# Preparation of weights and of v, held in its queue behind the step of g that precedes it in the source

## The chip, the core and the metric

The kernel runs on one core of a Trainium2 chip. The metric is the device time of one execution in microseconds (us), here the median of the runs shown. A core has TensorE (matrix products), VectorE, ScalarE and GpSimd (work on tiles), SyncE (starts most transfers) and DMA engines that carry them. Each engine works through its own queue of instructions in order; an instruction that has to wait holds up all that stand behind it in that queue.

## The reference

An attention over pooled keys and values feeds a gated layer, and that a second layer (4608 tokens of 512):

```python
k_p = k.reshape(B, H, Sp, pool, D).mean(axis=3)          # pool = 8: 576 keys become 72
v_p = v.reshape(B, H, Sp, pool, D).mean(axis=3)
scores = scale * np.matmul(q, k_p.transpose(0, 1, 3, 2))
scores = scores - np.max(scores, axis=-1, keepdims=True)
attn = np.exp(scores)
attn = attn / (np.sum(attn, axis=-1, keepdims=True) + 1e-09)
x = np.matmul(attn, v_p)              # then laid out as [B * S, H * D] = [4608, 512]
a = x @ w1; b = x @ w2                # 512 -> 1024
x = ((a * b) @ w3) @ w_out            # 1024 -> 1024 -> 512
h = x @ w_in                          # 512 -> 2048
r = np.maximum(h, 0.0); g = r * r
out = g @ w_out2                      # 2048 -> 512
```

## The kernel before, in words

Every product of 32-bit numbers is made of three matmuls on rounded halves: an operand is written as hi (rounded) plus lo (the rounded rest), and hi x hi, hi x lo and lo x hi are summed. Rounding thus costs one copy on ScalarE (hi) and one difference on VectorE (lo), here `split` (lines 119 and 120 in the profile) or lines of its own.

In the first 105 us `fold` multiplies w3 by the first w_out into one matrix W, Wt in the profile. Then, up to 828 us, nine blocks of 512 tokens run through the first layer. Each has eight steps: `stage_ab` makes the sums with w1 and w2 (ps_w) and from them the step of g: `asb`, ScalarE's copy of the sum with w1; `gf`, VectorE's product with the other sum; `gt`, the rounding of gf. `stage_w`, two steps later, multiplies gt by W into the sums acc. The attention of the eight batches is spread between these matmuls: scores ps_s, exp (att, line 482), the rest rem of a group, transposes ps_t that are rounded to aT and aR, and the products ps_av with the rounded pooled v (vl, and vr for what does not fill 128 rows), from which x is rounded (lines 543 and 546).

The second layer follows from 818 us. Its products are made in Strassen's manner, with seven products of quarters in place of eight, for four pairs of blocks and a plain ninth block: `h_step` multiplies x2o by units of weights, un, that are fetched from memory into a ring of eight. Its quarters of weights, their sums and differences are prepared beforehand and stored. One set of this preparation (`make_quarters`) loads two tiles (raw or rq), turns each with two scalings on ScalarE (`words`, lines 150 and 151) and three operations on VectorE (`join`, lines 159 to 162) into wq, makes the sums sq (lines 896 to 900), rounds all into oq (lines 910 and 914) and stores them. `second_half` does the like for the second halves of w1 and w2 (w32, wt2, lines 1289 and 1293) and `parted` rounds v (lines 359 and 360). The operands of the first pair, x2o, are rounded from x2r, which is loaded (line 1059) from the outputs x2d of the first layer; `cut` makes some differences of x2r first (line 1071).

raw, rq, x2r and the tiles of k and v share a pool of three buffers. wq, sq and oq share one of four. A load waits until the last reader of the buffer's old content is done, and it waits in SyncE's queue, in front of all that stand behind it.

The source issues all of this in one interleaved order (`tick` lets a pump issue a next piece of attention or of preparation after every six matmuls), but it does not fix the queues: a scheduler orders each engine's queue by the dependencies and its own model of when things get ready. An edge without a semaphore can be added between two instructions of one engine, as `issue_after` does: the first then has to stand ahead of the other. Before, `behind` uses this alone for the sums that pool k and v (lines 322 and 326), which stand behind `front["dve"]`, the last gf or Wt of the source.

## Time and profile before

| | us |
|---|---|
| median of 3 runs | 1529.75 (1527.83 to 1531.23) |
| the profiled execution | 1530.1, of which the trace spans 1528.3 |
| TensorE busy | 1488.6 (97%) |
| VectorE busy | 1001.5 (66%) |
| ScalarE busy | 798.3 (52%) |
| GpSimd busy | 83.6 (5%) |

A busy TensorE is one with a matmul in flight; weights are loaded beside that. The profile gives for each engine the idle time ahead of an instruction and what ended it. `issue` there means that the profile shows nothing that it waited for. The granted clock is 1.00 where TensorE ran at 2.4 GHz and 0.50 where it ran at 1.2 GHz.

### The profile page before, as it was taken

How to read it: one execution, taken by the hardware profiler on the slowest of the kernel's cores; microseconds unless marked ns; L12 is line 12 of the kernel's file. 1: busy time of each engine (PE TensorE's matmuls, PEld its weight loads, DVE VectorE, ACT ScalarE, POOL GpSimd, SP SyncE). 2: the span in 40 equal slices, each digit the busy share in tenths (PEclk: the TensorE clock that was granted, in tenths of full speed). 3: DMA queues.
4: the chain of work that ended last, by engine and by line, in shares of the span. 5: the costliest groups of instructions: out<-in, count | busy, mean ns of one | idle time of the engine just before them, and what ended most of it. 6: DMA issues, size and time to landing. Idle time of an engine off the chain costs nothing.

```text
span 1528.3 us, 21310 instructions
## 1 busy us (share of the span) xinstructions
PE 1488.6 (97%) x6752; PEld 1197.6 (78%) x6752; DVE 1001.5 (66%) x1798; ACT 798.3 (52%) x1953; POOL 83.6 (5%) x144
## 2 busy tenths in 40 slices
PE   5899999999999999999999999999999999999998
PEld 3457778787888887878888878888888888888887
DVE  7988686667757467657255476759675967576542
ACT  6866464454635345546244574457445744464441
POOL 1011111111110011100000000000000000000000
PEclk9999999999999999999999999999999999999999
DMA  9544666667676557648439777778777777798752
GB/s 295 190 139 138 165 201 164 188 158 203 169 198 177 172 130 211 205 140 263 136 126 306 217 203 231 207 209 231 235 207 206 234 206 207 207 268 283 209 162 90
DMA packets 292783, 301.34 MB, mean 197 GB/s; under 512 B 119360, under 2 KB 184896, under 8 KB 292672
## 3 DMA queue, kind: packets, MB, share of 16 engines
q1 hardware_dynamic: 287488, 290.54, 65.9%
q10 hardware_dynamic: 5184, 9.44, 1.7%
q8 instruction: 55, 0.90, 0.3%
q14 instruction: 56, 0.46, 0.1%
HBM read 243.27 MB, written 56.62 MB: 196 GB/s over the span
## 4 chain that ended last, share of the span: by engine, by line
PE 78%; DVE 10%; DMA 4%; ACT 4%; issue 2%; SPq 1%; ACTq 0%; DVEq 0%
PE ps_w L192 21%; PE o L1202 18%; PE acc L192 10%; PE ps_a L1100 5%; PE ps_c L1100 5%; PE ps_d L1100 5%; PE ps_h L192 3%; PE o L192 3%; PE ps_b L1100 3%; PE ps_s L465 2%; PE ps_av L192 1%; ACT att L482 1%; DVE gt L120 1%; DVE vp L326 1%; DVE raw L160 1%
## 5 line engine op out<-in xcount | busy, mean ns | idle before, releaser
L1202 PE MATMUL o<-gt,un 128*128 128x512 f32 x1344 | 330.1, 390 | 1.4 <-DVE gt L120 1.0
L1202 PEld LDWEIGHTS o<-gt,un 128*128 128x128 f32 x1344 | 251.8, 188 | 56.0 <-DVE gt L120 3.5
L120 DVE TENSOR_TENSOR gt<-gs,gt 128x512 fp32r<-128x512 f32 x240 | 164.7, 689 | 183.1 <-ACT gt L119 181.6
L192 PE MATMUL ps_w<-x,wt 128*128 128x512 f32 x960 | 243.5, 399 | 1.7 <-DVE x L546 0.9
L119 ACT CAST gt<-gs 128x512 fp32r<-128x512 f32 x240 | 148.6, 620 | 154.5 <-PE o L1202 89.3
L192 PE MATMUL acc<-gt,Wt 128*128 128x512 f32 x864 | 216.3, 394 | 0.0
L192 PEld LDWEIGHTS ps_w<-x,wt 128*128 128x128 f32 x960 | 175.7, 189 | 40.8 <-DVE x L546 2.6
L192 PEld LDWEIGHTS acc<-gt,Wt 128*128 128x128 f32 x864 | 159.9, 188 | 31.9
L192 PE MATMUL ps_w<-x,un 128*128 128x512 f32 x768 | 184.3, 393 | 0.0
L192 PEld LDWEIGHTS ps_w<-x,un 128*128 128x128 f32 x768 | 142.7, 188 | 29.6 <-issue 0.4
L482 ACT ACTIVATE att<-ps_s,mx 128x72 f32<-128x72 f32 (+1 forms) x320 | 97.9, 323 | 50.4 <-DVE mx L480 50.0
L1107 ACT ACTIVATE r<-r 128x512 f32<-128x512 f32 x96 | 60.7, 632 | 118.4 <-DVE r L1137 117.9
L827 DVE TENSOR_TENSOR gf<-asb,ps_w 128x512 f32<-128x512 f32 x72 | 49.3, 684 | 83.7 <-PE ps_w L192 75.2
L1100 PE MATMUL ps_a<-x2o,un 128*128 128x512 f32 x384 | 98.0, 390 | 0.1
L1100 PE MATMUL ps_c<-x2o,un 128*128 128x512 f32 x384 | 97.6, 390 | 0.0
L1100 PE MATMUL ps_d<-x2o,un 128*128 128x512 f32 x384 | 97.5, 389 | 0.0
L1108 ACT ACTIVATE gs<-r 128x512 f32<-128x512 f32 x144 | 90.0, 629 | 4.3 <-DMA x2r<-x2d 2.6
L1176 DVE TENSOR_TENSOR gs<-gs 128x512 f32<-128x512 f32 x128 | 86.6, 684 | 0.0
L119 ACT CAST gt<-gf 128x512 fp32r<-128x512 f32 x72 | 44.9, 623 | 75.4 <-DVE gf L827 75.3
L1100 PEld LDWEIGHTS ps_a<-x2o,un 128*128 128x128 f32 x384 | 72.0, 188 | 15.5 <-ACT p L1125 0.6
L1100 PEld LDWEIGHTS ps_c<-x2o,un 128*128 128x128 f32 x384 | 72.0, 188 | 15.2 <-DVE u L1131 0.3
L1100 PEld LDWEIGHTS ps_d<-x2o,un 128*128 128x128 f32 x384 | 72.1, 188 | 15.0
(113 smaller groups left out, 1969.5 us busy)
## 6 DMA issues: line engine op xcount, KB each, us to landing
un<-u_w SPq DMA_DIRECT2D x128, 256.0 KB, 3.2
un<-u_A SPq DMA_DIRECT2D x128, 256.0 KB, 3.0
un<-u_S SPq DMA_DIRECT2D x128, 256.0 KB, 3.0
un<-u_oS SPq DMA_DIRECT2D x128, 256.0 KB, 3.0
un<-u_oA SPq DMA_DIRECT2D x96, 256.0 KB, 3.0
raw<-in_moe_w_dram SPq DMA_DIRECT2D x32, 512.0 KB, 5.2
raw<-in_moe_w_out_dram SPq DMA_DIRECT2D x24, 512.0 KB, 4.5
kv<-in_k_dram SPq DMA_DIRECT2D x32, 256.0 KB, 3.4
```

The lines of the kernel that those rows point to most:

```text
L119: nc.scalar.copy(hi, src)
L120: return (eng or nc.vector).tensor_sub(lo, src, f32(hi))
L160: nc.vector.scalar_tensor_tensor(u, hi, 0x80000000, lo, op0=ALU.bitwise_and, op1=ALU.bitwise_or)
L192: (lambda a=a, b=b, i=i: nc.tensor.matmul(ps, a, b, start=first and i == 0, stop=last and i == n - 1))
L465: nc.tensor.matmul(ps[:n, x * 2 * SP:(x + 1) * 2 * SP], t[:, hp, c0:c0 + n], kbd[:, hp].rearrange("p a s -> p (a s)"), start=True, stop=True)
L482: nc.scalar.activation(av[:, h0 + h], sv[:, h], ACTF.Exp, bias=mx[:n, h:h + 1], scale=scale, accum_out=sm[:n, h0 + h:h0 + h + 1])
L827: front["dve"] = nc.vector.tensor_mul(gf, asb, pss[1])
L1100: nc.tensor.matmul(ps, l, r, start=first and j == 0, stop=j == len(todo) - 1, skip_group_check=True)
L1107: nc.scalar.activation(t, src, ACTF.Relu)
L1108: nc.scalar.activation(take(name), t, ACTF.Square)
L1176: d = nc.vector.tensor_sub(src, a, src)
L1202: nc.tensor.matmul(ob[x][o], l, r, start=u == 0 and m != 5 and j == 0, stop=u == NU - 1 and j == 2, skip_group_check=True)
```

## The change

`front` gets a second entry, for ScalarE, and `behind` is called with the engine. `front["act"]` is the last asb copy, and after it the hi copy of gt; `front["dve"]` is the last gf (or Wt), and after it the lo difference of gt. The scalings, the first instruction of each join, the roundings of v but for line 372, the sums of a set (the first of each half) and the roundings of wt2 and oq get an edge behind the entry that stands there when the source issues them. The rounding of gt is written out, without `split`, so that its two instructions can be entered. In the profile after, lines from 150 on stand one to three further down.

```diff
-    def behind(ins):
-
-        if "dve" in front:
-            issue_after(ins, front["dve"])
+    def behind(ins, eng="dve"):
+
+        if eng in front:
+            issue_after(ins, front[eng])
+        return ins
...
-        nc.scalar.activation(hf, hf, ACTF.Copy, scale=2.0 ** -112)
-        nc.scalar.activation(w.bitcast(U32), r[:, :, 0], ACTF.Copy, scale=2.0 ** -29)
+        behind(nc.scalar.activation(hf, hf, ACTF.Copy, scale=2.0 ** -112), "act")
+        behind(
+            nc.scalar.activation(w.bitcast(U32), r[:, :, 0], ACTF.Copy, scale=2.0 ** -29), "act")
...
-        nc.vector.tensor_scalar(lo, hi, 3, None, op0=ALU.logical_shift_left)
+        behind(nc.vector.tensor_scalar(lo, hi, 3, None, op0=ALU.logical_shift_left))
...
-            nc.scalar.activation(hi, src, ACTF.Copy, scale=row)
-            nc.vector.scalar_tensor_tensor(
-                lo, src, row, f32(hi), op0=ALU.mult, op1=ALU.subtract)
+            behind(nc.scalar.activation(hi, src, ACTF.Copy, scale=row), "act")
+            behind(nc.vector.scalar_tensor_tensor(
+                lo, src, row, f32(hi), op0=ALU.mult, op1=ALU.subtract))
...
-                nc.scalar.copy(asb, ps)
+                front["act"] = nc.scalar.copy(asb, ps)
...
         front["dve"] = nc.vector.tensor_mul(gf, asb, pss[1])
-        split(gt[:, 0, :], gt[:, 1, :], gf)
+        front["act"] = nc.scalar.copy(gt[:, 0, :], gf)
+        front["dve"] = nc.vector.tensor_sub(gt[:, 1, :], gf, f32(gt[:, 0, :]))
...
-                nc.vector.tensor_add(s1, a21, quarter(w, 1, 1))
+                behind(nc.vector.tensor_add(s1, a21, quarter(w, 1, 1)))
...
-                nc.vector.tensor_sub(s3, a11, a21)
+                behind(nc.vector.tensor_sub(s3, a11, a21))
...
-            nc.scalar.copy(order(t[:, 0, :]), natural(part(n)))
+            behind(nc.scalar.copy(order(t[:, 0, :]), natural(part(n))), "act")
...
-            nc.vector.tensor_sub(
-                order(t[:, 1, :]), natural(part(n)), order(f32(t[:, 0, :])))
+            behind(nc.vector.tensor_sub(
+                order(t[:, 1, :]), natural(part(n)), order(f32(t[:, 0, :]))))
...
-            nc.scalar.copy(t[:, 0, :], st_["w"])
+            behind(nc.scalar.copy(t[:, 0, :], st_["w"]), "act")
...
-            nc.vector.tensor_sub(t[:, 1, :], st_["w"], f32(t[:, 0, :]))
+            behind(nc.vector.tensor_sub(t[:, 1, :], st_["w"], f32(t[:, 0, :])))
```

What this does to the queues is seen at three places. Numbers behind a name tell one buffer's use from another.

First place, ScalarE's queue near 300 us of the trace, before: two scalings of a weight's second tile, rq_2922, stand ahead of the attention's rounding aT0_2892 and its exps (att).

```order
L150 ACTIVATE rq_2919<-rq_2919 128x512
L151 ACTIVATE wq_3014<-rq_2919 128x512
L482 ACTIVATE att1_105,sm_2947<-ps_s_2943,mx_2946 128x72 x4
L910 CAST oq_3108<-wq_3014 128x512
L823 COPY asb_2972<-ps_w1_2954 128x512
L150 ACTIVATE rq_2922<-rq_2922 128x512
L151 ACTIVATE wq_3014<-rq_2922 128x512
L119 CAST aT0_2892<-ps_t_3003 128x4x128
L482 ACTIVATE att1_105,sm_2947<-ps_s_2987,mx_2990 128x72 x4
L119 CAST gt_3018<-gf_3017 128x512
```

The same stretch of ScalarE's queue in the changed kernel.

```order
L484 ACTIVATE att1_105,sm_2947<-ps_s_2943,mx_2946 128x72 x4
L825 COPY asb_2972<-ps_w1_2954 128x512
L151 ACTIVATE rq_2919<-rq_2919 128x512
L153 ACTIVATE wq_3014<-rq_2919 128x512
L830 CAST gt_3018<-gf_3017 128x512
L119 CAST aT0_2892<-ps_t_3003 128x4x128
L484 ACTIVATE att1_105,sm_2947<-ps_s_2987,mx_2990 128x72 x4
L859 COPY st_3025<-acc0_2240 128x512
L859 COPY st_3031<-acc1_2241 128x512
L860 DMA x2d1_107<-st_3025 128x512
```

The scalings of rq_2922 have left the stretch (they stand twelve rows further down, behind another group of exps); those of rq_2919 and gt_3018 stand ahead of aT0_2892 now, and the rounding oq_3108 has gone down as well.

Second place, VectorE before: the joins of set 5's tiles raw_7798 and raw_7800 into wq_8015, during the attention of the last batch, some 100 us before the first layer ends.

```order
L914 TENSOR_TENSOR oq_7774<-sq_7711,oq_7774 128x4x4x32
L914 TENSOR_TENSOR oq_7796<-sq_7711,oq_7796 128x4x4x32
L159 TENSOR_SCALAR raw_7798<-raw_7798 128x512
L160 SCALAR_TENSOR_TENSOR raw_7798<-raw_7798 128x2x256
L159 TENSOR_SCALAR raw_7800<-raw_7800 128x512
L162 ISA wq_8015<-raw_7798,wq_8015 128x1024
L160 SCALAR_TENSOR_TENSOR raw_7800<-raw_7800 128x2x256
L162 ISA wq_8015<-raw_7800,wq_8015 128x1024
L914 TENSOR_TENSOR oq_8079<-wq_8015,oq_8079 128x4x4x32
```

VectorE in the changed kernel, around the same joins.

```order
L831 TENSOR_TENSOR gt_8042<-gf_8041,gt_8042 128x512
L161 TENSOR_SCALAR raw_7798<-raw_7798 128x512
L162 SCALAR_TENSOR_TENSOR raw_7798<-raw_7798 128x2x256
L161 TENSOR_SCALAR raw_7800<-raw_7800 128x512
L164 ISA wq_8015<-raw_7798,wq_8015 128x1024
L162 SCALAR_TENSOR_TENSOR raw_7800<-raw_7800 128x2x256
L164 ISA wq_8015<-raw_7800,wq_8015 128x1024
L120 TENSOR_TENSOR x2o_7831<-x2r_7853,x2o_7831 128x512
L1074 TENSOR_TENSOR x2r_7850<-x2r_7853,x2r_7850 128x512
L120 TENSOR_TENSOR x2o_7832<-x2r_7830,x2o_7832 128x512
L829 TENSOR_TENSOR gf_8104<-asb_8085,ps_w2_8087 128x512
L120 TENSOR_TENSOR x2o_7823<-x2r_7856,x2o_7823 128x512
```

They now stand behind the last step of g but one (gt_8042), and the roundings of the second layer's operands (x2o) and the differences of x2r stand behind them. Before, all x2o of this list stood at least 20 rows ahead of gt_8042.

SyncE before: the loads of x2r_7853 and x2r_7856 into the buffers that these joins read, with the stores of set 4 (u_oS) ahead of them.

```order
L961 DMA u_oS3_4_8011<-oq_7796 256x1x256
L961 DMA u_oS4_4_8013<-oq_7796 256x1x256
L1059 DMA x2r_7853<-x2d0_106 128x512
L1059 DMA x2r_7853<-x2d1_107 128x512
L1059 DMA x2r_7856<-x2d0_106 128x512
L1059 DMA x2r_7856<-x2d1_107 128x512
L961 DMA u_oA11_5_8154<-oq_8079 256x1x256
```

SyncE in the changed kernel, with those loads and the fetches (un) of the second layer's units around them.

```order
L964 DMA u_oS3_4_8011<-oq_7796 256x1x256
L964 DMA u_oS4_4_8013<-oq_7796 256x1x256
L234 DMA un_8018<-u_A11_0_2201 128x512
L234 DMA un_8020<-u_S2_0_2494 128x512
L234 DMA un_8037<-u_S1_0_2490 128x512
L234 DMA un_8039<-u_S3_0_2532 128x512
L1062 DMA x2r_7853<-x2d0_106 128x512
L1062 DMA x2r_7853<-x2d1_107 128x512
L1062 DMA x2r_7856<-x2d0_106 128x512
L1062 DMA x2r_7856<-x2d1_107 128x512
L234 DMA un_8081<-u_A12_0_2286 128x512
L234 DMA un_8083<-u_S4_0_2536 128x512
```

Six fetches stand between the stores and the loads now that came after the loads before, and further fetches stand behind them.

Third place, TensorE near 680 us before: the attention's products ps_av_6942 between matmuls of W on gt_6822.

```order
L192 MATMUL acc0_6441<-gt_6822,Wt_994 128x512 x2
L192 MATMUL ps_av_6942<-aT0_6692,vl_101 128x256
L192 MATMUL ps_av_6942<-aT1_6693,vl_101 128x256
L465 MATMUL ps_s_6952<-kbd_103,qT_6320 128x144 x2
L192 MATMUL acc0_6441<-gt_6822,Wt_994 128x512
L192 MATMUL acc1_6442<-gt_6822,Wt_994 128x512 x2
L192 MATMUL ps_av_6942<-aT0_6692,vl_101 128x256
L192 MATMUL acc1_6442<-gt_6822,Wt_994 128x512
L530 MATMUL ps_av_6942<-aR_6694,vr_102 128x256
L192 MATMUL acc2_6443<-gt_6822,Wt_994 128x512 x3
L192 MATMUL ps_w1_7005<-x_7_0_6120,wt_430 128x512
```

TensorE in the changed kernel, the same stretch.

```order
L194 MATMUL acc3_6444<-gt_6822,Wt_994 128x512 x2
L194 MATMUL ps_av_6942<-aT0_6692,vl_101 128x256
L194 MATMUL ps_av_6942<-aT1_6693,vl_101 128x256
L467 MATMUL ps_s_6952<-kbd_103,qT_6320 128x144 x2
L194 MATMUL ps_av_6942<-aT0_6692,vl_101 128x256
L194 MATMUL acc3_6444<-gt_6822,Wt_994 128x512
L194 MATMUL acc0_6441<-gt_6902,Wt_1043 128x512 x3
L194 MATMUL acc1_6442<-gt_6902,Wt_1043 128x512 x3
L194 MATMUL acc2_6443<-gt_6902,Wt_1043 128x512 x3
L194 MATMUL acc3_6444<-gt_6902,Wt_1043 128x512 x3
L532 MATMUL ps_av_6942<-aR_6694,vr_102 128x256
L194 MATMUL ps_w1_7005<-x_7_0_6120,wt_430 128x512
```

The products with vl (aT) come after nearly all of gt_6822's; behind them follow all twelve matmuls of the next step, gt_6902, then the product with vr, and at once the first one that needs x of it (x_7_0).

## Rows read from the trace of the kernel before

**Rows 1.** Stretches: us, then PE, PEld, DVE, ACT, POOL busy, clock, DMA share, GB/s.
```profile
96.00:330.00 234.00, 224.70 (x1065) 176.43 (x1063) 171.19 (x341) 128.48 (x423) 30.60 (x50) 0.99 0.59 165
330.00:820.00 490.00, 486.58 (x2318) 400.46 (x2317) 299.17 (x603) 233.81 (x708) 40.31 (x69) 1.00 0.63 182
900.00:1528.00 628.00, 622.35 (x2738) 513.09 (x2736) 409.82 (x630) 316.11 (x540) 0.00 (x0) 1.00 0.74 212
```

**Rows 2.** TensorE's waits, 96 to 330 us: operation, line, releaser: total, times, longest.
```profile
PE ps_t L517 <- issue: 2.7, 2, 2.4
PE ps_av L192 <- DVE x L546: 1.3, 2, 0.9
PE ps_av L192 <- DVE aT L120: 0.7, 1, 0.7
PE ps_s L465 <- ACT qT L418: 0.6, 1, 0.6
```

**Rows 3.** TensorE's waits, 330 to 820 us.
```profile
PE ps_s L465 <- ACT att L482: 0.7, 1, 0.7
PE ps_av L192 <- ACT vl L359: 0.6, 1, 0.6
PE ps_av L192 <- DVE vl L360: 0.6, 1, 0.6
```

**Rows 4.** Time line, 284 to 306 us: start, duration, operation, count [idle before].
```profile
294.67 0.69 DVE L827 TENSOR_TENSOR gf<-asb,ps_w 128x512 f32<-128x512 f32 x1
...
299.02 0.65 ACT L150 ACTIVATE rq<-rq 128x512 f32<-128x512 f32 x1 [4.58 <-DMA rq<-in_moe_w_in_dram]
...
300.12 0.57 ACT L119 CAST aT<-ps_t 128x512 fp32r<-128x512 f32 x1
...
301.32 0.68 DVE L120 TENSOR_TENSOR aT<-ps_t,aT 128x512 fp32r<-128x512 f32 x1
...
302.01 0.51 PE L517 MATMUL ps_t<-ident,rem 128*96 128x128 f32 x2 [2.40 <-issue]
...
303.11 3.23 PE L192 MATMUL ps_w<-x,wt 128*128 128x512 f32 x8
```

**Rows 5.** Stretches by engine, with the granted clock, beside two of those waits.
```profile
145.00:147.00 2.00, 1.43 (x10) 1.13 (x10) 1.97 (x5) 2.00 (x13) 0.00 (x0) 1.00 0.68 255
302.00:304.00 2.00, 1.99 (x8) 1.90 (x9) 1.90 (x6) 1.58 (x4) 0.96 (x1) 0.54 0.08 14
```

**Rows 6.** Time line of TensorE, 144 to 147 us.
```profile
145.57 0.63 PE L512 MATMUL ps_t<-ident,att 128*128 128x128 f32 x4 [1.69 <-issue]
```

**Rows 7.** Time line of VectorE, 144 to 150 us.
```profile
147.53 1.50 DVE L1293 TENSOR_TENSOR wt<-w,wt 128x512 fp32r<-128x512 f32 x1
```

**Rows 8.** Time line of TensorE, 804 to 842 us: the passage to the second layer.
```profile
818.02 1.52 PE L1100 MATMUL ps_a<-x2o,un 128*128 128x512 f32 x6
...
826.18 2.88 PE L192 MATMUL acc<-gt,Wt 128*128 128x512 f32 x12
```

**Rows 9.** Time line of VectorE, 796 to 846 us.
```profile
808.57 0.43 DVE L159 TENSOR_SCALAR raw<-raw 128x512 uint32<-128x512 uint32 x1 [0.79 <-ACT wq L151]
...
809.51 0.69 DVE L160 SCALAR_TENSOR_TENSOR raw<-raw 128x512 uint32<-128x512 uint32 x1
810.23 0.69 DVE L162 CUSTOM_DVE_ANT_0 wq<-raw,wq 128x1024 uint16<-128x1024 uint16 x1
810.84 0.68 DVE L120 TENSOR_TENSOR gt<-gf,gt 128x512 fp32r<-128x512 f32 x1
```

**Rows 10.** All that reads or writes x2r: ns min/median/max, starts; last row its loads.
```profile
L119 ACT CAST x2o<-x2r x60: 603/618/627, 748.9 to 1347.0; 128x512 fp32r<-128x512 f32 x60
L120 DVE TENSOR_TENSOR x2o<-x2r,x2o x60: 678/683/693, 749.5 to 1348.1; 128x512 fp32r<-128x512 f32 x60
...
DMA to landing us min/median/max: 3.3/5.3/8.0
```

**Rows 11.** DMA issues that begin from 800 to 830 us: count, size, us to landing.
```profile
x2r<-x2d SPq DMA_DIRECT2D x5, 256.0 KB, 6.8
```

## What the change was predicted to do

> **What bounds the kernel now.** I read the stretches first, then TensorE's waits, then the time line at the places that the waits name. TensorE is the engine that ends the kernel. From 900 us on it is busy 622.35 of 628 us, and from 330 to 820 us 486.58 of 490 [rows 1]; no order of the other engines can give much there. From 96 to 330 us it is busy only 224.70 of 234. The groups of waits say what for: products of the attention wait for VectorE or ScalarE (x 1.3 us, aT 0.7, qT 0.6), and transposes (ps_t) wait 2.4 us in one place for nothing that the profile names [rows 2]. After 330 us three waits of 0.6 to 0.7 us interest here: for att, and twice for the rounded v, vl [rows 3]. VectorE and ScalarE have time to spare in every stretch [rows 1], so what counts is the place in their queues: an instruction that can't start yet holds up all that is queued behind it.
>
> The largest wait shows that. At 302.01 us TensorE had stood for 2.40 us. Its transposes needed the PSUM buffer that the step aT empties. ScalarE's half of aT began at 300.12 and VectorE's at 301.32, although ScalarE had nothing else to wait for: it stood 4.58 us on the first scaling of a weight (rq) whose load had not landed, with aT and four exps queued behind it [rows 4]. The idle time has a second price: the granted clock from 302 to 304 us is 0.54, so 1.2 GHz instead of 2.4 [rows 5], and eight matmuls take 3.23 us [rows 4], where twelve of the same shape take 2.88 elsewhere [rows 8], some 0.227 each and 0.16 for the last one's end.
>
> **What the change does, part by part.** It adds no instruction and removes none. The first instruction of each piece of preparation on ScalarE or VectorE (and the second scaling of a weight) gets an ordering edge behind the asb copy, gt copy, gf product or gt difference before it in the source. All queues are laid out anew, so I read the new order against the old times.
>
> *The wait at 302 us.* Now the asb copy, the words of the other tile, the gt copy and then aT and the exps precede the scaling of rq_2922 (first place in the section on the change). The gt copy needs gf, which VectorE made at 294.67 [rows 4], so it holds nothing. aT moves to about 296 us, and VectorE's half is no longer behind the joins. The 2.40 us go, and the slow clock with them: 3.23 - (8 x 0.227 + 0.16) = 1.25. What is late next is nothing within 3 us, since both inputs of the transposes are there at 296. I take -3.65, with -2.4 as the least.
>
> *The early waits.* The qT copies go ahead of the v casts, and VectorE's half of aT goes ahead of the rounding of wt2, which took 1.50 us just before it [rows 7]. That is worth 0.6 + 0.7 [rows 2] if nothing else is late; but the pooling of k now stands before the x steps there. Half: -0.65, between 0 and -1.3. *At 318 us* the longer wait for x (0.9) [rows 2] has a rounding of oq and sums ahead of it, which now follow x; yet the roundings of v and another gf now stand ahead. Half again: -0.45, between 0 and -0.9. *At 597 and 680 us* the casts of vr go behind the exps, and TensorE gets the rest of one W product and all of the next (12 matmuls; third place there) ahead of the remainder's product with vr, so the two waits for vl are filled; but then the first x of the next block follows at once, uncovered. Of 0.7 + 0.6 + 0.6 [rows 3] I take half, -0.95, between 0 and -1.9.
>
> Together -5.7, between -2.4 and -7.75.
>
> *The passage to the second layer, near 818 us.* Here the change costs. Before, the joins of the weights' set 5 follow set 4's roundings at once, the two raw buffers that they read are then filled with x2r, the first layer's output, and rounding that into the operands x2o begins at 748.9 us [rows 10]. Now that set's scalings and joins stand behind the last step of g but one of the whole layer (second place there, VectorE and SyncE). The difference gt_8042, at 810.84 before, no longer has 0.43 + 0.69 + 0.69 of joins ahead of it [rows 9], so ends near 809.7. Each operation there starts 0.08 us before the one ahead of it ends (810.84 against 810.23 + 0.69) [rows 9], so a join takes 0.35 + 0.61 + 0.61, and two follow: the first buffer is free at about 811.2, the second at 812.8. Only then can SyncE start x2r_7853 and x2r_7856, and the fetches queued behind them. Landing takes 3.3 to 8.0 us, 5.3 in the middle, over all loads of x2r [rows 10]; the five from 800 to 830 us took 6.8 [rows 11].
>
> By 5.3 us the first lands at 816.5 and ScalarE has rounded its first operand at 817.1. VectorE then works through 24 instructions of 0.68 us [rows 10], 0.61 apart, 14.6 us in a row. The lower half of x2o_7823 is the fifth, ready at 820.2. TensorE wants it 0.68 us (three matmuls) after the first product of h, which began at 818.02 [rows 8]: 1.5 late. x2o_7826 is six instructions later, 823.9. TensorE, after the rest of that product and one of W, wants its lower half at 822.05: 1.85 more. What follows (x2o_7827, gt_8105, 7829) is in time by then. So the W product that ended at 826.18 + 12 x 0.227 = 828.90 [rows 8] would end about 3.4 us late. Each microsecond of landing more or less moves both waits' sum by as much: +1.4 at 3.3 us, +4.9 at 6.8, +6.1 at 8.0. I take 5.3, which is the middle of the view with the most loads: +3.4.
>
> Those two waits are 1.5 and 1.85 us. A wait of 1.69 us at 145.57 [rows 6] left the clock at 1.00 in 145 to 147 us [rows 5], so I add nothing for the clock. The Trainium skill (TensorE: Matmul & The Clock Gate, section "Why this matters for your kernels") says that idle gaps between bursts of matmuls send the clock back to half rate, which speaks against this change; the trace agrees after 2.40 us of idle (0.54), not after 1.69 (1.00). By that rule alone the passage would cost 1.25 more, and the sum below would be about zero.
>
> *Behind it* the sets 6 and 7 and part of 5 now run while the first four units of h want the same two engines, and their loads and stores queue with the fetches on SyncE. No row shows such a mixture, so between 0 and +2; +0.6, since the engines' load there stays under that of TensorE. *New waits at the head of a queue*: a rounding can now be the first to wait for a store's buffer, ahead of an exp. The 4.58 us of before is the one such wait that I find under a wait of TensorE: 0 to +2, and I take +0.5.
>
> **Sum.** -5.7 + 3.4 + 0.6 + 0.5 = -1.2 us. The profiled execution took 1530.1 us (span 1528.3, 1.8 around it): 1528.9. The median of the three runs is 0.35 less, so the forecast is 1528.6 us. A measurement of this kernel can tell a difference of 0.2%, 3.06 us, from none.
>
> **Rivals.**
> *The passage is nearly free.* x2r lands in 3.3 us, the least that the view shows [rows 10]: +1.4, no added waits. -5.7 + 1.4 = -4.3, 1525.4. For it: with the stores of sets 5 to 7 later, the queues are emptier at 812 us than they were. Against: the fetches for h load at the same time. Chance 0.30.
> *The passage is expensive: slower.* It is one mechanism: x2r can't start before the joins end, and lands in traffic. From a landing of about 8 us on, with the sets behind it at their +2 and waits at +1, and the uncertain gains gone but for 302 us and the early ones (-4.3), it gives +6.1 + 2 + 1 - 4.3 = +4.8, 1534.5. For it: 6.8 us in that very stretch [rows 11]. Against: part of the traffic of that stretch were the stores that now come later. The Trainium skill (DMA: Bandwidth & Descriptors, "Latency and other measured facts") has HBM's latency grow with load, and calls it the main part of a transfer's fixed cost; the trace agrees, 3.3 at the least against 6.8 there. Chance 0.25.
> *The change doesn't do what it says.* Queues move, but the other waits come back at the next batch for other reasons: only -3.65 stays, and +3.4 + 0.6: no difference, 1530. Chance 0.10.
> The forecast itself has 0.35, with 1526.5 to 1531 as its own range.
>
> Faster takes the first rival and the forecast's lower edge, 0.33; slower the second and a bit of the forecast, 0.26; within 0.2% 0.41. The range leaves out some of the first rival's full gains (-7.75 + 1.4, 1523.4) and the largest sums on the other side: 1523.5 to 1534.8.
>
> **What the profile after would show.** At about 300 us no wait of TensorE over 1 us and a clock of 1.00; aT's copy near 296. The x2r loads near 812 us, and VectorE without a gap from about 817 to 832. TensorE waiting for x2o (or ScalarE's half of it) at the second operand of the first h product, and again at x2o_7826; the W product after them 2 to 5 us late against the rest. I am wrong if the passage shows no wait, if the waits there exceed 6 us, or if the first layer gains less than 3 us or more than 8 up to 810 us.

## The result

The changed kernel takes 1544.04 us (median of five runs, 1541.03 to 1546.15), the kernel before, run beside it, 1529.75 (1527.83 to 1531.23). The ratio is 1.0092, with a 95% interval of 1.0079 to 1.0104: 14.3 us slower, where 1.2 us faster was predicted. The prediction is wrong, and 1544 lies outside its range of 1523.5 to 1534.8.

In the profile after, the stretches that answer to [rows 1] (us, then PE, PEld, DVE, ACT, POOL busy, clock, DMA share, GB/s; the second layer is entered some 6 us later, so the same bounds cut off a little earlier work):

```profile
96.00:330.00 234.00, 222.96 (x1060) 172.77 (x1059) 165.85 (x336) 123.62 (x415) 29.12 (x47) 1.00 0.57 158
330.00:820.00 490.00, 483.85 (x2302) 396.91 (x2302) 273.11 (x559) 219.04 (x684) 39.06 (x71) 1.00 0.57 167
900.00:1542.00 642.00, 636.26 (x2800) 524.51 (x2798) 419.80 (x646) 326.61 (x558) 0.00 (x0) 1.00 0.73 214
```

TensorE idles 1.7 us more than before in the first stretch and 2.7 more in the second, where less idle time was forecast. Behind 900 us its idle time is the same 5.7 us as before. To place the loss I took the start of the same matmul (the n-th of the trace) in both traces; the difference is called the distance below. After lies behind before by 4.4 us at 295 (time of before), 1.9 at 321, 4.6 at 611, 6.0 at 805, 7.2 at 828, 11.9 at 851, 14.0 at 863, and by 14 from there to the end. So about 6 us were lost in the first layer, and 8 in the passage to the second. Each distance comes from one profile of each kernel, and the runs of before alone lie 3.4 us apart, so I take a difference of 2 to 3 us between two distances for scatter; that is an estimate.

The place at 302 us looks as forecast. Two stretches of after there:

```profile
300.00:302.00 2.00, 2.00 (x10) 1.65 (x9) 1.62 (x5) 2.00 (x10) 0.00 (x0) 1.00 0.30 83
302.00:304.00 2.00, 2.00 (x11) 1.58 (x10) 1.82 (x5) 1.60 (x6) 0.50 (x1) 1.00 0.14 54
```

TensorE is busy throughout at a clock of 1.00, where [rows 4, 5] had 2.40 us of idle time and 0.54; the distance falls from 4.4 to 1.9 across it. That the held scalings did this is not shown by after, though: it comes to this place 4.4 us late, and experiment e2 below, which is before with the new entries of `front` alone, holds no scaling, is 3.9 us late there and has no wait of TensorE either. In e2 the scaling of rq still waits for its load, with aT behind it:

```profile
300.52 0.67 ACT L151 ACTIVATE rq<-rq 128x512 f32<-128x512 f32 x1 [3.09 <-DMA rq<-in_moe_w_in_dram]
301.08 0.57 ACT L119 CAST aT<-ps_t 128x512 fp32r<-128x512 f32 x1
```

But TensorE now waits elsewhere. Its waits in after, from 60 to 330 us (operation, line, releaser: total, times, longest):

```profile
PE ps_t L514 <- issue: 3.3, 1, 3.3
PE ps_av L194 <- ACT vl L361: 1.9, 2, 1.4
```

and from 330 to 820 us:

```profile
PE ps_av L194 <- ACT vl L361: 1.9, 2, 1.7
PE ps_t L519 <- issue: 1.8, 2, 1.3
PE ps_av L532 <- ACT vr L374: 1.0, 2, 0.5
```

The waits for v's rounded halves (vl, vr) were to become shorter; in the second stretch vl went from 0.6 twice [rows 3] to 1.9, and vr is new.

### The profile page after: what moved, and what is told of

It reads as the page before. It is cut to its first block, busy times and chain, and to the rows that moved or that the text cites. A ratio compares the mean times of both kernels' runs of the same rounds, so it can differ in the third digit from the quotient of the medians.

```text
span 1542.2 us, 21277 instructions
## 1 busy us (share of the span) xinstructions
PE 1493.0 (97%) x6752; PEld 1195.7 (78%) x6752; DVE 995.4 (65%) x1798; ACT 795.9 (52%) x1953; POOL 80.8 (5%) x144
## 4 chain that ended last, share of the span: by engine, by line
PE 74%; DVE 12%; ACT 5%; DMA 5%; issue 2%; SPq 1%; POOL 0%; ACTq 0%; DVEq 0%; POOLq 0%
PE ps_w L194 21%; PE o L1205 18%; PE acc L194 8%; PE ps_a L1103 5%; PE ps_c L1103 5%; PE ps_d L1103 4%; PE ps_h L194 3%; PE o L194 3%; PE ps_b L1103 2%; PE ps_s L467 2%; DVE vp L328 1%; PE ps_av L194 1%; DMA raw<-in_moe_w_dram 1%; DVE raw L162 1%; ACT att L484 1%
## 5 line engine op out<-in xcount | busy, mean ns | idle before, releaser
L825 ACT COPY asb<-ps_w 128x512 f32<-128x512 f32 x72 | 42.4, 589 | 100.7 <-PE ps_w L194 100.5
```

The lines of the kernel that those rows point to most:

```text
L825: front["act"] = nc.scalar.copy(asb, ps)
```

## Where the first layer lost its time

The edit moves one step that the prediction gave no term: the pooling of k and v (`total`, lines 324 and 328 after). Its reductions already stood behind `front["dve"]`. That entry was gf; now it is gt's difference, which needs ScalarE's copy of gt first. VectorE's time line of after near 680 us (start, duration, line, operation [idle before]):

```profile
678.76 0.43 DVE L161 TENSOR_SCALAR raw<-raw 128x512 uint32<-128x512 uint32 x1 [2.56 <-ACT wq L153]
...
679.83 0.68 DVE L829 TENSOR_TENSOR gf<-asb,ps_w 128x512 f32<-128x512 f32 x1
680.43 0.68 DVE L164 CUSTOM_DVE_ANT_0 wq<-raw,wq 128x1024 uint16<-128x1024 uint16 x1
681.20 0.69 DVE L831 TENSOR_TENSOR gt<-gf,gt 128x512 fp32r<-128x512 f32 x1
681.81 1.07 DVE L328 TENSOR_REDUCE vp<-kv 128x64 f32<-128x512 f32 x1
682.79 0.68 DVE L917 TENSOR_TENSOR oq<-wq,oq 128x512 fp32r<-128x512 f32 x1
683.39 1.01 DVE L328 TENSOR_REDUCE vp<-kv 128x64 f32<-128x512 f32 x1
```

ScalarE in the same stretch:

```profile
681.19 0.63 ACT L913 CAST oq<-wq 128x512 fp32r<-128x512 f32 x1
684.44 0.91 ACT L361 ACTIVATE vl<-vp,rows 128x256 fp32r<-128x256 f32 x2 [2.62 <-DVE vp L328]
```

The last two poolings wait out a join, gf, another join, gt and a rounding, and the rounding of v, and TensorE, wait for them. And it closes a ring: the pooling is the last reader of a buffer of the shared pool, so a late one makes the next load of v late. The loads and poolings of the last v in before, in after, and in the kernel of experiment e18, which is after with the pooling let go and with no edges in the last block, a fence each:

```profile
L318 SPq DMA_DIRECT2D kv<-in_v_dram x4: 333/363/611, 600.8 to 666.6; - x4
L326 DVE TENSOR_REDUCE vp<-kv x4: 1060/1068/1089, 665.5 to 675.9; 128x64 f32<-128x512 f32 x4
```

```profile
L320 SPq DMA_DIRECT2D kv<-in_v_dram x4: 333/352/423, 604.3 to 676.2; - x4
L328 DVE TENSOR_REDUCE vp<-kv x4: 1010/1056/1067, 672.3 to 683.4; 128x64 f32<-128x512 f32 x4
```

```profile
L329 DVE TENSOR_REDUCE vp<-kv x4: 1071/1072/1092, 607.9 to 646.3; 128x64 f32<-128x512 f32 x4
L321 SPq DMA_DIRECT2D kv<-in_v_dram x3: 332/334/423, 609.0 to 643.6; - x3
```

(Duration min/median/max in ns, first and last start.) The last pooling starts at 675.9 us in before, at 683.4 in after, which is some 6 us late there in all, and at 646.3 in e18. So most of the 37 us between after and e18 is not the move: in before, too, the pooling stands behind a step of g, and it is late there as well. e18 takes off the old edge together with the moved one.

## Where the passage lost its time

The first part is the crowd that the prediction described. The loads of x2r issue from 817.53 us and land after about 3 us, ScalarE rounds six operands at once, and VectorE works from 821.24 to 838 with one gap of 0.17. ScalarE, VectorE and TensorE in after, a fence each:

```profile
820.59 3.23 ACT L119 CAST x2o<-x2r 128x512 fp32r<-128x512 f32 x6 [1.24 <-DMA x2r<-x2d]
```

```profile
821.24 0.69 DVE L120 TENSOR_TENSOR x2o<-x2r,x2o 128x512 fp32r<-128x512 f32 x1 [2.45 <-ACT x2o L119]
...
829.94 3.09 DVE L120 TENSOR_TENSOR x2o<-x2r,x2o 128x512 fp32r<-128x512 f32 x5
...
836.03 0.68 DVE L1131 TENSOR_TENSOR u<-ps_b,p 128x512 f32<-128x512 f32 x1
```

```profile
827.11 0.50 PE L1103 MATMUL ps_b<-x2o,un 128*128 128x512 f32 x1 [0.91 <-ACT x2o L119]
```

TensorE pays only 0.91 us for it there; the distance is up by 1.2 at 828. The rest comes behind the crowd. VectorE reaches the first sum of h (u) at 836.03; in before, where TensorE is 7 us ahead, it does at 823.02:

```profile
823.02 0.68 DVE L1128 TENSOR_TENSOR u<-ps_b,p 128x512 f32<-128x512 f32 x1
```

The steps that follow on ScalarE in after then share its queue with what the edges have put off, roundings (L913) and scalings (L151, L153):

```profile
841.15 0.63 ACT L1111 ACTIVATE gs<-r 128x512 f32<-128x512 f32 x1 [1.90 <-DMA raw<-in_moe_w_out_dram]
841.69 0.60 ACT L913 CAST oq<-sq 128x512 fp32r<-128x512 f32 x1
...
845.81 0.64 ACT L151 ACTIVATE raw<-raw 128x512 f32<-128x512 f32 x1
...
846.87 0.65 ACT L153 ACTIVATE wq<-raw 128x512 uint32<-128x512 uint32 x1
847.41 0.57 ACT L1128 COPY p<-ps_a 128x512 f32<-128x512 f32 x1
```

The copy p empties the PSUM buffer ps_a that TensorE's next product needs. TensorE, and the granted clock of two stretches:

```profile
848.04 2.33 PE L1103 MATMUL ps_a<-x2o,un 128*128 128x512 f32 x6 [2.17 <-ACT p L1128]
850.17 2.47 PE L1103 MATMUL ps_b<-x2o,un 128*128 128x512 f32 x6
852.48 0.85 PE L1103 MATMUL ps_c<-x2o,un 128*128 128x512 f32 x3
```

```profile
844.00:848.00 4.00, 1.86 (x9) 1.19 (x7) 1.14 (x3) 4.00 (x9) 0.00 (x0) 1.00 1.04 402
848.00:852.00 4.00, 3.96 (x11) 3.11 (x12) 3.99 (x8) 3.06 (x6) 0.00 (x0) 0.60 1.08 390
```

A wait of 2.17 us, then a granted clock of 0.60: most of those 4 us at 1.2 GHz. Twelve matmuls take 852.48 - 848.04 = 4.44 us; at the 0.227 us of the full clock, 2.72. So this one place costs 2.17 + 1.72 = 3.9 us. Shorter waits for steps of h (0.87 at 857.61, 0.81 at 870.96, 0.55 at 873.89) follow. With the 0.91 us these are 7.0 of the 8 us.

## The experiments

Each ratio is against the kernel before, run on the same chip, with its 95% interval; it can differ by 0.1% from that of the medians. 0.2% is 3.06 us. Behind it stand two distances as above, in us: the one at the end of the first layer (before's 805 us; after has 6.0), and what the passage adds up to 897 (after: 8.0). In the expectations V says that the held rounding of v costs the first layer, P that the pooling's edge does, Q that the second layer's sets of weights do, K that their raw buffers are kept longer, R that the held roundings and sums crowd the engines, H that edges or held work stand in the queues ahead of the pooling and rounding of v. S says that sets beside the first units of h cost the passage, L that the late loads of x2r alone do.

**e1.** Before, with the new fronts and only the rounding of v held (after without these edges):

```diff
-        behind(nc.scalar.activation(hf, hf, ACTF.Copy, scale=2.0 ** -112), "act")
+        nc.scalar.activation(hf, hf, ACTF.Copy, scale=2.0 ** -112)
...
-        behind(nc.vector.tensor_scalar(lo, hi, 3, None, op0=ALU.logical_shift_left))
+        nc.vector.tensor_scalar(lo, hi, 3, None, op0=ALU.logical_shift_left)
...
-            behind(nc.scalar.copy(order(t[:, 0, :]), natural(part(n))), "act")
+            nc.scalar.copy(order(t[:, 0, :]), natural(part(n)))
```

> The kernel before, with the fronts of the changed one (asb, gt's copy, gf, gt's difference) and only the rounding of v held behind them; weights are prepared as before. Theory V (the held rounding of v makes the attention's products late; it costs the first layer some 6 us or more): 1534 to 1538 us, and TensorE waits for vl or vr for 4 us or more in all from 200 to 700 us. Rival P (it is the pooling of k and v, which now stands behind gt's difference instead of gf): the same time as the kernel with the fronts alone. Rival Q (held weights cost it): 1530 us, no more waits for v than before (about 1.5 us).

1531.31 against 1528.55, ratio 1.0019 (1.0010 to 1.0028); distance -0.4 and +1.1. The rounding of v is not the loss. (The pooling stands behind gt's difference here too; e15 below takes that away.)

**e2.** As e1, and the rounding of v free too, so that of the whole change only the fronts are left: the pooling stands behind gt's difference.

```diff
-            behind(nc.scalar.activation(hi, src, ACTF.Copy, scale=row), "act")
+            nc.scalar.activation(hi, src, ACTF.Copy, scale=row)
```

> The kernel before, with the fronts of the changed one, and nothing held but what was held before, the pooling of k and v, which so stands behind gt's difference instead of gf. V and Q: 1529 to 1531 us, no change. P: 1533 to 1536 us, with the pooled sums (line 328) and so vl later by one wait for ScalarE's copy of gt.

1.0041 (1.0026 to 1.0056), distance 3.0, passage -0.6. An edge that the source's diff shows only as a new entry of a table costs 6.3 us alone by the ratio; by medians (1533.02 against 1528.55) it is 4.5, and by the profile, which is of the fastest of five runs, 2.4. Most of e2's distance is there by 200 us (2.5), and its largest wait from 96 us on is the one for ps_t that after has at 147 us:

```profile
146.99 1.09 PE L513 MATMUL ps_t<-ident,att 128*128 128x128 f32 x4 [3.60 <-issue]
```

Before has 1.69 there [rows 6].

**e3.** After, with all second-layer sets free.

```diff
-                run_step(quarters)
+                run_free(quarters)
```

> The changed kernel, but the sets of the second layer's weights are issued without an edge to g. The passage to the second layer should be as before: none of the 8 us lost from 820 to 900 us. First layer: V 1534 to 1538 us (6 us lost still, and the wait for the rq load near 300 us, 2.4 us, is back); Q 1529 to 1531 us.

1.0020 (1.0010 to 1.0030): most of the loss is gone, -0.5 and -0.2, though the pooling still stands behind gt's difference. The wait at 302 us, which V had back, did not come back; as in e2, TensorE gets there late (2.1 us).

**e4.** After, without edges in the last block.

```diff
-        if eng in front:
+        if eng in front and hold[0]:
...
+        hold[0] = i < last
```

> The changed kernel, but from the last block of the first layer on nothing is held. Theory S (the passage costs 8 us because the sets 5 to 7 are prepared beside the first units of the second layer): 1535 to 1537 us, the distance to the kernel before is 6 us at 820 us and still 6 to 7 us at 900. Rival L (the late loads of x2r alone cost it; or another order of the second layer's instructions): 1541 to 1544 us, the distance grows by 5 us or more from 820 to 900 us.

1.0049 (1.0034 to 1.0064), 4.8 and +0.2, near S's numbers and far from L's. The passage is paid for by the last block's edges: 0.92 - 0.49 = 0.43%, 6.6 us by the ratios. But e4 also rounds x2o early again, so it doesn't tell the sets from x2o.

**e5 and e6.** After with the scalings and joins of the sets free, sums and roundings held; and the converse.

```diff
-            words(st_["r", x], st_["w"][:, x])
+            free(words, st_["r", x], st_["w"][:, x])
...
-            join(st_["r", x], st_["w"][:, x])
+            free(join, st_["r", x], st_["w"][:, x])
```

```diff
-                behind(nc.vector.tensor_add(s1, a21, quarter(w, 1, 1)))
+                nc.vector.tensor_add(s1, a21, quarter(w, 1, 1))
...
-            behind(nc.scalar.copy(order(t[:, 0, :]), natural(part(n))), "act")
+            nc.scalar.copy(order(t[:, 0, :]), natural(part(n)))
```

> The changed kernel, but in the sets of the second layer's weights the scalings and joins, which read the shared raw buffers, have no edge to g; sums and roundings keep theirs. Theory K (raw buffers held longer make the loads of k and v, and so vp and vl, late; that is what the first layer loses by the held sets, 5 us): at 820 us the distance to the kernel before is 0 to 1.5 us, and no wait for vl over 1.2 us. Rival R (the held roundings and sums crowd the engines where v is rounded): at 820 us 4 to 6 us late, as the changed kernel. From 820 to 900 us it still loses 3 to 8 us in either theory, since roundings stay behind g: 1533 to 1538 us by K, 1538 to 1543 by R.

> The reverse: in the sets the scalings and joins are held behind g as in the changed kernel, sums and roundings are not. K: at 820 us 4 to 7 us late, waits for vl of 1.5 us and over at 317 and 685 us stay; with the passage 1541 to 1545 us. R: at 820 us under 2 us late; 1536 to 1539 us.

e5 1.0041 (1.0026 to 1.0056), 3.9 and +1.2; e6 1.0081 (1.0066 to 1.0096), 6.1 and +5.4. K, which wanted 0 to 1.5 in e5's first layer, is missed, and R, which wanted under 2 in e6's, is missed too: either held half leaves a loss of 4 to 6 us. The passage of 3 to 8 us that both had for e5 did not come either, and that speaks against S: four joins and twelve roundings of sets still stand behind the last gf, and it costs almost nothing. What differs is that the raw buffers come free early, and x2o is rounded before the units begin. In e6's passage TensorE never waits for p: its two long waits, 1.15 us at 848.66 and 1.39 at 861.27, are for fetched units (un), which share SyncE's queue with the late loads and stores.

**e7.** After, with a piece of a set every second tick.

```diff
-    rate_q = [3]
+    rate_q = [2]
```

> The changed kernel with the sets issued at every second tick of the source instead of every third, so that all are done before the last block of the first layer. S: nothing is lost from 820 to 900 us (distance within 1 us at both). K: the first layer loses as much or more, 5 to 9 us, as more raw tiles are under way beside the loads of k and v: 1535 to 1539 us. If what matters is only how late the sets end, it comes out near the kernel before, 1528 to 1531 us.

1.0071 (1.0054 to 1.0088), 7.4 and -0.6: the sets are done earlier, the passage is free and the first layer is not.

**e8.** e2 with ScalarE's scalings held as well.

```diff
-        nc.scalar.activation(hf, hf, ACTF.Copy, scale=2.0 ** -112)
+        behind(nc.scalar.activation(hf, hf, ACTF.Copy, scale=2.0 ** -112), "act")
...
```

> The kernel before with the fronts of the changed one and only the scalings on ScalarE held (of all weights), no join, sum, rounding of weights or v. K: the scalings alone keep the raw buffers, so 4 to 7 us late at 820 us, and the passage costs some 6 to 8 us: 1540 to 1545 us, nearly all of the loss by 144 of the held instructions. R: under 2 us late at 820 us, 1532 to 1538 us.

1.0076 (1.0061 to 1.0091), 4.4 and +4.2. That is 0.35% over e2: the first layer as K has it, the passage less than its 6 to 8.

**e9 to e12.** Two buffers of their own for k and v, to cut the ring through the shared pool; room for them from a ring of six fetches in place of eight. e9 is after with that ring alone, e10 after with both, e11 before with both, e12 is e3 with both.

```diff
-RING = 8
+RING = 6
...
+            if kvp and not (src is v and j == NP):
+                pool, tag = kvp[0], "kv"
```

> The changed kernel with a ring of six units in place of eight: it frees 4 KB per partition, and is the control for the next. If the ring is no limit in the first layer, at 820 us as late as the changed kernel (6 us, 5 to 7); the second layer may lose by later fetches: 1542 to 1550 us.

> The same ring of six, and from the second block on the loads of k and v (but for v's remainder) have two buffers of their own instead of three shared with the weights. Theory K (held preparation keeps the shared raw buffers, by the scalings or by the four buffers of wq, sq and oq behind them, and so delays v's loads): against the control the first layer gains 3 us or more by 820 us, the last batch's v loads start 5 us or more earlier, waits for vl at 317 and 685 us under 1 us. Rival H (the held instructions stand in ScalarE's and VectorE's queues ahead of the pooling and rounding of v): less than 1.5 us of gain, waits for vl stay over 1.2 us.

> The kernel before with the ring of six and the own buffers for k and v. K: shared buffers cost it little, so within 1.5 us of the kernel before at 820 us; the second layer as far behind as the control loses by its ring. If it gains 2 us or more by 820 us, the sharing was a cost already before.

> The changed kernel with the second layer's sets free of the edges, the ring of six and the own buffers: the candidate for a faster version. 1524 to 1529 us if the own buffers take off what is left of the waits for v (some 3 us) and the smaller ring costs nothing; 1530 to 1534 otherwise.

e9 1.0119 (1.0100 to 1.0139), e10 1.0102 (1.0087 to 1.0117), e11 1.0104 (1.0087 to 1.0121), e12 1.0159 (1.0143 to 1.0175). e9 is 3.2 us late at 805, where 5 to 7 was expected. Against e9, e10 gains 2.9 us in the first layer, about the scatter; but two buffers cost the kernel before 11.7 us there, where K had 1.5 at most, so they are no neutral cut. Not conclusive, and e12, the candidate for a faster kernel, is the slowest of all.

**e13.** After, with the pooling and the rounding of v free.

```diff
-            behind(nc.vector.reduce_sum(
-                dst(j)[:n], raws[j][:n].rearrange("p r d -> p d r"), axis=AX.X))
+            nc.vector.reduce_sum(
+                dst(j)[:n], raws[j][:n].rearrange("p r d -> p d r"), axis=AX.X)
...
-            behind(nc.scalar.activation(hi, src, ACTF.Copy, scale=row), "act")
+            nc.scalar.activation(hi, src, ACTF.Copy, scale=row)
```

> The changed kernel, without edges for the pooling of k and v and for the rounding of v; weights stay held. If buffers delay the loads of v (K): little changes, at 820 us 3 to 6 us late, the last batch's v loads still at 672 us or later and the waits for vl near 685 us still over 1.2 us; 1541 to 1545 us. If their own edges delay pooling and rounding (H): 3 us or more better at 820 us, 1537 to 1540 us.

1.0029 (1.0019 to 1.0040), but -6.4 in the first layer and +10.2 in the passage. H holds and K falls; the gain in the first layer is larger than H had it. This kernel lacks the edge of the pooling altogether, the one of before too. The pattern at ScalarE repeats in the passage: a wait of 1.82 us for a load at 828.77, then a queue without a gap until p at 835.04, on which TensorE waits 2.1 us. Two more waits, 2.71 at 845.60 and 1.97 at 861.50, are for VectorE's sums r.

**e14.** After, with a piece at 5 of 14 ticks: fewer joins and roundings are left behind the last gf than in e5 (2 and 7), while nine of fourteen x2o are still late.

```diff
-        if ring and quarters and not operands and ticks[0] % rate_q[0] == 0:
+        if ring and quarters and not operands and (
+                ticks[0] % 14 in (0, 3, 6, 9, 12) if rate_q[0] == 3 else ticks[0] % rate_q[0] == 0):
```

> The changed kernel with the sets issued at 5 of 14 ticks instead of 1 of 3, so that they end a set earlier: x2o stays as late (9 of its 14 roundings behind the last gf, 11 in the changed kernel), but 2 joins and 7 roundings of weights stand behind it instead of 4 and 12. If the crowd of x2o operands is what the passage costs: 5 us or more lost from 810 to 900 us. If the sets beside the units are: 1.5 to 3.5 us. If only both together, between these, 3.5 to 5.

1.0059 (1.0041 to 1.0076), -1.5 and +10.4. Fewer sets beside the units and a passage as dear as after's: the late x2o goes with the cost, the sets alone don't. ScalarE and TensorE of e14 where most is lost:

```profile
851.19 0.62 ACT L913 CAST oq<-sq 128x512 fp32r<-128x512 f32 x1 [3.33 <-DMA u_oA<-oq]
...
853.80 0.56 ACT L1128 COPY p<-ps_a 128x512 f32<-128x512 f32 x1
```

```profile
854.42 2.93 PE L1103 MATMUL ps_a<-x2o,un 128*128 128x512 f32 x6 [3.09 <-ACT p L1128]
```

Here it is a rounding that waits 3.33 us for the store of its buffer, with h's steps and p behind it. In e5 ScalarE's roundings wait 6.5 us for such stores between 812 and 870, and TensorE waits only 1.0 in the passage. I read this as such a wait costing where the chain of h is already late; no run tests it alone.

**e15 and e16.** e1 with the pooling and VectorE's half of v left behind gf; ScalarE's half behind gt's copy (e15) or asb (e16).

```diff
-        front["dve"] = nc.vector.tensor_sub(gt[:, 1, :], gf, f32(gt[:, 0, :]))
+        nc.vector.tensor_sub(gt[:, 1, :], gf, f32(gt[:, 0, :]))
```

> The kernel before, with only the rounding of v held: on ScalarE behind gt's copy, on VectorE behind gf, and the pooling behind gf as it was. 1525 to 1528 us if what e2 lost (0.4%) came from the pooling behind gt's difference and what e1 won against e2 (0.2%) from the held rounding of v; 1528 to 1531 if the orders only scatter.

> As the one ahead, with ScalarE's rounding of v behind the asb copy only, not gt's. The same two cases: 1525 to 1528, or 1528 to 1531 us.

0.9987 (0.9976 to 0.9997) and 0.9993 (0.9983 to 1.0002). e1 and e15 differ by that one front, the pooling and VectorE's half of v behind gt's difference or behind gf: 1.0019 against 0.9987, 0.32%, and 3.87 against 1.68 us for the wait for ps_t near 146 us. So the move has a price of 0.3 to 0.4% here as in e2. Holding the rounding of v with the pooling behind gf is worth 0.13% (0.03 to 0.24), and -4.0 us at 805.

**e17 and e18.** After, pooling free, no edges in the last block; the rounding of v free (e17) or held (e18, so that e4 and e18 differ by the pooling's edge alone).

```diff
-        if eng in front:
+        if eng in front and hold[0]:
...
-            behind(nc.vector.reduce_sum(
+            nc.vector.reduce_sum(
```

> The changed kernel with edges for the weights alone (pooling and rounding of v are free), and none from the last block of the first layer on. If what e13 gained in the first layer (6.4 us against the kernel before) and what e4 saved in the passage (8 us) stand beside each other: 1521 to 1525 us, faster than both kernels. If the passage costs again, or the gain was scatter: 1527 us or more.

> As the one ahead, but with the rounding of v held as in the changed kernel; the pooling stays free. If the pooling's edge is what costs the first layer: within 2 us of the one ahead. If the rounding's own edge is: 3 to 6 us more, and waits for vl or vr of over 1 us near 317, 600 or 685 us.

e17: 1525.09 against 1529.26, 0.9972 (0.9962 to 0.9982); e18: 0.9974 (0.9963 to 0.9984). Both are faster than before and than after; e18 is 0.75% under e4, 11.5 us for the pooling's edge with the weights held. But before has such an edge too, behind gf. No run takes it from before alone, and none holds the weights with the pooling behind gf, so what these two gain over before is not shown to come from the held weights. In e17, from 330 to 820 us, no wait for vl is left under TensorE:

```profile
PE ps_t L515 <- issue: 1.3, 1, 1.3
PE ps_av L533 <- ACT vr L375: 0.7, 1, 0.7
PE ps_s L468 <- ACT att L485: 0.4, 1, 0.4
```

## Why the prediction was wrong, point by point

*What bounds the kernel* was read rightly: the order of the two queues under TensorE's waits decides. Kernels that differ by ordering edges alone run from 1524.9 us (e18) to 1544.0.

*302 us and the sum of the gains, -5.7.* The first layer lost 6.0. Whether the mechanism at 302 us holds, after can't show, since it gets there late. The kernels that get there in time speak for it: from 295 to 321 us, e13, e17 and e18, with the scalings held, gain 4.6 to 5.3 us and have no wait there, while e15 and e16, with the scalings free, gain 1.5 and 1.9 and keep waits of 1.62 and 1.21. The sum looks right in e13 (-6.4 in the first layer) and e17 (-5.0; the whole kernel -4.2 by medians), but these lack the pooling's old edge too, and e15 has -4.0 without any held weight, so that is no proof of it.

*The first step that failed is one with no term in the sum: the pooling.* The prediction asked what each edited line moves, and took the pooling of k only as a neighbour of the early x steps. It did not ask who else reads `front["dve"]`. The distances at 805 us put the parts side by side: -4.0 with the rounding of v held and the pooling behind gf (e15), -0.4 with the pooling behind gt's difference (e1), -0.5 with all of the change but the edges of the sets (e3), 6.0 with these too (after), 4.8 without the edges of the last block (e4), and -5.6 if the pooling's edge goes as well (e18). So the loss takes both, the sets held and the pooling behind a step of g. By the ratios, from e18 over e4 to after: -0.26% with the weights and v held, +0.75% for the pooling's edge, +0.43% for the last block's edges, which is -4.0 + 11.5 + 6.6 us. The 11.5 us are for the whole edge; its move from gf to gt's difference cost 5 to 6 us with free weights (e2, and e1 against e15), and with held ones it was not measured by itself. That held roundings and joins crowd the place where the pooling now stands is my reading of the time line at 680 us; no run tests it alone.

*The early waits and those at 597 and 680 us* were forecast to shrink by half. The waits for qT, aT and att did go, and the longest for x at ps_av fell from 0.9 to 0.3, but one of 0.9 for aR came. Those for vl grew instead, to 1.74 at 685 us, which is the pooling (e4 has the same, e18 none). And a wait that the prediction used for the clock alone and gave no term, the one for ps_t at 145.57 of 1.69 [rows 6], grew to 3.27. The moved pooling by itself does that: the wait is 3.60 in e2, and 3.87 in e1 against 1.68 in e15.

*The passage, +3.4, and the sets behind it, +0.6,* were right in kind and mis-sized: 4.0 forecast, 8.0 by the profile, 6.6 by the ratios. The first load landed in 3 us, not 5.3, but issued at 817.53, not 811.2, behind a first layer that was 6 us late itself. Of the two waits for x2o, 1.5 and 1.85, one came, of 0.91, at the second product of h. (The 822.05 behind the second doesn't follow from the rows shown: three matmuls and a product of W behind 820.2 give 823.6, and a second wait of 0.3.) What was missing is what comes behind the crowd on VectorE: u at 836.03, and then ScalarE's queue, in which p stands behind the delayed sets. The prediction followed x2o to the product that needs it and stopped there. That the late x2o goes with the cost is shown (after, e6, e8, e13 and e14 against e4, e5 and e7). By which way it costs is not: after waits for p, e13 for p and for VectorE's r, e6 for fetched units, and no run tells VectorE's crowd from ScalarE's waits for loads and stores.

*New waits at the head of a queue, +0.5,* is the term next to it. After has one of 1.90 us for a load at 841.15 and e14 one of 3.33 for a store, each ahead of p. Such waits cost TensorE little in e5.

*No clock cost.* This failed with the 2.17 us wait: 1.7 us more. By the rule that the prediction set against its row, it would have been 1.25. That rule, of the Trainium skill (TensorE: Matmul & The Clock Gate, section "Why this matters for your kernels"), was taken without the length of gap that the page sets for it; taken so, the trace agrees with it at 848 us (0.60 after 2.17 us) and not at 147 us (1.00 after 3.27 us), below.

*The rivals.* The expensive passage (1534.5) came nearest, and was given 0.25; none contained the pooling. Of the signs that were to show me wrong, one appeared plainly: the first layer gained less than 3 us. The waits in the passage were 5.3 us by themselves, and 7.0, over the 6 of the other sign, with the slow clock.

## What to carry to other kernels

When a shared marker changes its meaning, list every reader of it and cost each one's move, not only the lines of the diff. When an experiment lets such a reader go altogether, ask whether the kernel before had held it too: its gain is then not the price of the move. And a place where a wait has gone proves little in a kernel that comes there late. Where a step that empties a shared buffer is put off, follow the ring: the next load, its reader, and the step that waits for that. Last, a burst of late work is followed through to the steps that it pushes back, until TensorE's PSUM buffers, not only to the product that needs its result.

## What the runs showed of the hardware

The length of one wait did not tell here whether the clock fell. After 2.17 us of idle time the granted clock was 0.60 (848 to 852 us of after), and after 3.09 us e14 had 0.50:

```profile
854.00:858.00 4.00, 3.58 (x9) 2.81 (x10) 2.08 (x3) 0.96 (x2) 0.00 (x0) 0.50 1.04 378
```

But the wait of 3.27 us at 147.09 us in after left it at 1.00, as did waits of 2.13 and 2.71 us in the passage of e13:

```profile
147.09 0.63 PE L514 MATMUL ps_t<-ident,att 128*128 128x128 f32 x4 [3.27 <-issue]
```

```profile
145.00:147.00 2.00, 0.00 (x0) 0.00 (x0) 2.00 (x5) 2.00 (x11) 0.00 (x0) 1.00 0.76 190
147.00:149.00 2.00, 1.91 (x11) 1.52 (x12) 2.00 (x4) 2.00 (x10) 0.00 (x0) 1.00 0.66 228
```

At the same place, e2 had 0.50 after 3.60 us:

```profile
147.00:149.00 2.00, 2.00 (x7) 1.73 (x8) 2.00 (x4) 1.98 (x10) 0.00 (x0) 0.50 0.68 237
```

So the prediction's inference from one wait of 1.69 us without a drop was not safe.
